# Transposes by halves of the rows, two score buffers, another order of the first loads and a logit sum by a product, in a fused attention and mixture-of-experts kernel

## The chip, the cores and the metric

The kernel runs on one core of a Trainium2 chip. The metric is the device time of one execution, in microseconds. Engines are named as in the profile: PE is TensorE (matrix products; PEld are its weight loads), DVE is VectorE, ACT is ScalarE, POOL is GpSimd, SP is SyncE, which only issues DMA transfers. PSUM is the memory into which TensorE writes, eight banks of 128 partitions by 512 floats; VectorE and ScalarE read it.

## What is computed

The input is `q`, `k`, `v` of shape (8 batches, 8 heads, 576 positions, 64). Attention is local: each head's positions are cut into 9 chunks of 64, and a chunk attends only to itself. The result, 4608 tokens of 512 features, goes through a mixture of 8 experts in which an expert keeps at most `capacity` = 80 tokens, those with the largest gate weight.

```python
scores = scale * np.matmul(q_c, k_c.transpose(0, 1, 2, 4, 3))   # per chunk of 64
attn = np.exp(scores - np.max(scores, axis=-1, keepdims=True))
attn = attn / (np.sum(attn, axis=-1, keepdims=True) + 1e-09)
x = np.matmul(attn, v_c)                  # then (batch, position) x (head, feature)
...
logits = x @ w_gate
expert_idx = np.argmax(logits, axis=1)
gate_w = probs[np.arange(N), expert_idx]
for e in range(E):
    tok_idx = np.where(expert_idx == e)[0]
    if len(tok_idx) > capacity:
        tok_idx = tok_idx[np.argpartition(-gate_w[tok_idx], capacity)[:capacity]]
    h = np.maximum(x[tok_idx] @ w1[e], 0.0)
    out[tok_idx] = gate_w[tok_idx, None] * (h @ w2[e])
```

## The kernel before

**Stages.** First comes the attention loop, over 36 units of 128 tokens with all 8 heads. Then follows a stretch in which the last gate weights are worked out and, for each expert, the tokens above its threshold are found and put in order (the tail). Then come six rounds of expert products, each on 128 slots, with the expert weights arriving by DMA; the results are scattered to the output rows. The other output rows are written with zeros.

**One unit.** `load(i)` issues the DMA transfers of unit i: queries (256 KB) and, in two halves, keys and values (258 KB each). Keys and values stand in one of seven buffers `kvb`; only the odd or the even partitions of each half are ever loaded, and the rest must be zero, so all seven buffers are zeroed once at the start. `scores(i)` multiplies queries by keys into PSUM (eight products of 128 rows by 64 columns, which appear as 16 instructions since each is done in two passes); VectorE takes the maximum of each row (L322) and subtracts it (L325), which gives `sm`. `probs(i)` transposes `sm` on TensorE, four transposes of 128 by 128 (L336) into one PSUM bank, and ScalarE takes the exponential from there (L338). `values(i)` multiplies by the values (L356), and VectorE normalises (L363 to L367) into `x`. `xtrans(i)` transposes `x`, again four transposes of 128 by 128 (L388) into a bank of its own, and ScalarE copies the result to `xT` (L389).

**Order of the work.** The order on each engine is that of the program text, written by hand. Pass i of the loop issues `scores(i)`, `probs(i-1)`, `values(i-2)`, `xtrans(i-3)` and the loads of unit i+5, so four units are under way at once. After each fourth unit `gate_mm`, `gate_copy` and `gate_sum` work out the logits of four units: the gate weights stand in four groups of 32 columns, one for each quarter of the features, and the four partial logits must be summed. `gate_sum` transposes them (L421), and VectorE sums the four parts (L425). What follows on the logits (maximum, exponential, key; `gate`) is put into a queue `gates`, and the search for each expert's threshold into a queue `bounds_q`; `fill()`, which is called five times in a unit, issues one step of the first and two of the second between the VectorE instructions of the unit. Some of these steps are ScalarE activations: the counts of the key search (`search_count`, L570, three rounds of two) and the level counts (`signs`, L504).

**PSUM.** Of the eight banks, scores have two (the loop uses one of them, one buffer), transposed probabilities one (`pt`), transposed `x` one (`m`), values two (`o`), and the gating two buffers of one bank (`g`).

**Start.** The seven buffers are zeroed first (L738: four on VectorE, three on GpSimd), then unit 0 is loaded, then VectorE zeroes `warm` (L742), on which TensorE does 14 products so that its clock comes up (`warm_up`, L747), then the other loads and constants follow. A product that needs zeros or data waits for them by semaphore.

**Tail.** After the loop the last four units of `x` are transposed (L388), the last two of them into the two halves of one tile of two banks; then the logits of the last eight units, the counts, the mask and the ranks follow, mostly one after the other.

Of the kernel before, what the change touches and what calls it, by code (L numbers as in the profile page):

```python
# [8 lines left out]
F32 = mybir.dt.float32  # L9
# [22 lines left out]
NWARM = 14  # L32
# [26 lines left out]
NCONST = C_V3 + 3  # L59
# [3 lines left out]
def attention_moe(ctx: ExitStack, tc: tile.TileContext, q, kv, wg, w1, w2, cap, cst, out):  # L63
# [20 lines left out]
    comp = cp.tile([P, RT, 6, NE], BF16, name="comp")  # L84
# [44 lines left out]
    def compact(pool, pp, ptok, tag):  # L129

        cand = pp.tile([P, 5, NE], F32, name=f"cand{tag}", tag="cand")
        for rt in range(RT):
# [4 lines left out]
                rhs=comp[:, rt, 0:5].rearrange("p c e -> p (c e)"),  # L137
# [129 lines left out]
    with ExitStack() as actx:  # L267
# [28 lines left out]
        def load(i):  # L296

# [7 lines left out]
            nc.sync.dma_start(t, q[T, r])  # L305
            for h in range(2):
                (nc.scalar if i < 2 and h else nc.sync).dma_start(kb[h:P:2, h], kv[T, r, h])

        def scores(i):
# [3 lines left out]
            ps = ps1.tile([P, 4, P], F32, name=f"s{i}", tag="s")  # L313
# [16 lines left out]

        def probs(i):
            d = U[i]
            pt = ps1.tile([P, 4, P], F32, name=f"pt{i}", tag="pt")
            sv = d['sm'].rearrange("p c k h -> p c (k h)")
            for pr in range(4):
                nc.tensor.transpose(pt[:, pr, :], sv[:, pr, :], ident)  # L336
            pT = wk.tile([P, 4, P], F32, name=f"pT{i}", tag="pT")
            nc.scalar.activation(pT, pt, AF.Exp, scale=0.125)  # L338
            d['pT'] = pT

        def values(i, last=False):
# [10 lines left out]
            po = ps1.tile([P, 2, 512], F32, name=f"o{i}", tag="s" if last else "o")  # L352
            for pr in range(4):
                o = 130 * (pr % 2)
                for u in range(2):
                    nc.tensor.matmul(  # L356
                        po[64 * u:64 * u + 64, pr // 2, o:o + 130].rearrange(
# [4 lines left out]
            pov = po[:, :, 0:260].rearrange("p j (m x) -> p j m x", m=4)  # L362
            nc.vector.tensor_scalar(rc, pov[..., 64], 1e-9, None, op0=ALU.add)  # L363
# [3 lines left out]
            nc.vector.tensor_tensor(  # L367
                t['x'][:, r, :].rearrange("p (j m e) -> p j m e", j=2, m=4), pov[..., 0:64],
                rc[:, :, :, None].to_broadcast([P, 2, 4, 64]), op=ALU.mult)
# [12 lines left out]
        def xtrans(i, pm=None):  # L382
            T, r = divmod(i, 4)
            t = TT[T]
            if pm is None:
                pm = ps1.tile([P, 4, P], F32, name=f"px{i}", tag="m")
            for pr in range(4):
                nc.tensor.transpose(pm[:, pr, :], t['x'][:, r, P * pr:P * pr + P], ident)  # L388
            nc.scalar.copy(t['xT'][:, :, P * r:P * r + P], pm)  # L389

        def gate_mm(rt, n):
            t = TT[rt // 4]
            U[rt]['pl'] = pls = []
            banks = ((ps2, "g"),) if rt < HALVES else ((ps2, "g"), (ps1, "m"))
            w = P * n // len(banks)
            for j, (pool, tag) in enumerate(banks):
# [339 lines left out]
        with tc.manual_schedule():  # L736
# [19 lines left out]
            for n in range(1, 4):  # L756
                load(n)
# [386 lines left out]
```

## Time and profile before

| | us |
|---|---|
| three runs | 274.03, 275.99, 277.04 (median 275.99) |
| the profiled execution, its own time | 273.62 |
| its span, first to last instruction | 271.4 |
| TensorE busy in it | 246.6 |
| VectorE busy | 134.7 |
| ScalarE busy | 77.5 |
| GpSimd busy | 55.2 |

In the rows of the timeline the first number is the start in microseconds from the start of the span, the second the duration (of the whole merged run of instructions where a row stands for several, x4 for instance), then come engine, line of the kernel, operation, output and inputs, and shapes. In brackets stands how long the engine had been idle before, and what released it. For TensorE the shapes are those of the stationary operand (rows by columns) and of the moving one. Rows by stretch give the busy time of each engine in the stretch, with the count of its instructions, TensorE's granted clock as a share of full speed, the busy share of the 16 DMA engines (up to about 1.04 is seen) and what they moved in GB/s. Grouped rows give the count, the busy time in all, the mean of one in ns, and the idle time before them with its cause.

### The profile page before, as it was taken

Reading aid. Unit: us, or ns where it says so; the run is one execution under the profiler, and the core shown is the slowest. Engines: PE = TensorE matmul, PEld = TensorE weight load, DVE = VectorE, ACT = ScalarE, POOL = GpSimd, SP = SyncE. Lnnn points to the kernel's source line nnn. Section 1 sums busy time; section 2 is a strip of 40 time slices with the busy share of each in tenths; the row PEclk is TensorE's granted clock in tenths of the full one; section 3 lists DMA queues with packets and bytes.
Section 4 is the critical chain, followed back from the end, with each engine's and each line's share of the span. In section 5 each row is a group of like instructions: output and inputs, shape, how many; then the busy total and the mean of one; then the engine's idle time right before and its main releaser. Section 6 shows DMA issues by size and latency. Waiting matters only on the chain. (4 is left out here: it accounts for less than half of the span.)

```text
span 271.4 us, 6612 instructions
## 1 busy us (share of the span) xinstructions
PE 246.6 (91%) x2703; PEld 148.9 (55%) x2703; DVE 134.7 (50%) x419; ACT 77.5 (29%) x159; POOL 55.2 (20%) x115
## 2 busy tenths in 40 slices
PE   0579999999999999999998878999999999999970
PEld 0458777777767687787876667342343434233320
DVE  7348758686767869695873867121121112112210
ACT  1003433433443554375755330220020202001000
POOL 9020101102020203069023453500000011110011
PEclk9999999999999999999999999999999999999996
DMA  4998799989998899979999971899999999996001
GB/s 145 381 282 294 250 323 386 347 280 315 390 341 315 278 342 318 378 261 391 395 408 408 331 297 44 295 368 406 404 393 408 407 403 393 407 387 244 0 36 35
DMA packets 32755, 84.71 MB, mean 312 GB/s; under 512 B 3344, under 2 KB 3472, under 8 KB 32720
## 3 DMA queue, kind: packets, MB, share of 16 engines
q1 hardware_dynamic: 28960, 71.32, 71.6%
q0 software_dynamic: 3456, 12.32, 13.0%
q10 hardware_dynamic: 304, 0.59, 0.6%
q8 instruction: 23, 0.38, 0.6%
q14 instruction: 12, 0.10, 0.1%
HBM read 64.04 MB, written 20.45 MB: 311 GB/s over the span
## 5 line engine op out<-in xcount | busy, mean ns | idle before, releaser
L202 PE MATMUL hc<-w,xtc 128*32 128x512 f32 x384 | 44.2, 594 | 0.2 <-ACT xtc L192 0.2
L235 PE MATMUL yc<-w,htc 128*32 128x512 f32 x384 | 43.4, 593 | 0.1
L316 PE MATMUL s<-kv,q 128*64 128x128 f32 x576 | 40.0, 282 | 1.8 <-POOL capc L768 1.7
L356 PE MATMUL o<-kv,pT 128*64 128x130 f32 x576 | 39.7, 279 | 0.0
L322 DVE TENSOR_REDUCE mx<-s 128x8 f32<-128x512 f32 x36 | 24.8, 690 | 22.4 <-PE s L316 22.3
L316 PEld LDWEIGHTS s<-kv,q 128*64 128x64 f32 x576 | 31.4, 138 | 8.3 <-issue 5.8
L356 PEld LDWEIGHTS o<-kv,pT 128*64 128x64 f32 x576 | 31.1, 135 | 5.9 <-issue 5.9
L338 ACT ACTIVATE pT<-pt 128x512 f32<-128x512 f32 x36 | 21.5, 597 | 35.1 <-PE pt L336 34.8
L235 PEld LDWEIGHTS yc<-w,htc 128*32 128x32 f32 x384 | 12.5, 110 | 29.2 <-issue 28.2
L202 PEld LDWEIGHTS hc<-w,xtc 128*32 128x32 f32 x384 | 12.1, 110 | 26.0 <-issue 25.6
L367 DVE TENSOR_TENSOR x<-o,rc 128x512 f32<-128x512 f32 x36 | 24.8, 689 | 0.8 <-DMA xs<-x 0.2
L325 DVE TENSOR_TENSOR sm<-s,mx 128x512 f32<-128x512 f32 x36 | 24.8, 690 | 0.6
L389 ACT COPY xT<-px 128x512 f32<-128x512 f32 x32 | 18.6, 581 | 22.1 <-PE px L388 22.0
L336 PE MATMUL pt<-ct,sm 128*128 128x128 f32 x144 | 23.5, 286 | 0.0
L388 PE MATMUL px<-ct,x 128*128 128x128 f32 x144 | 22.7, 283 | 0.8 <-ACT kv L389 0.8
L241 POOL DMA_INDIRECT out<-ysc,si x6 | 6.0, 995 | 84.8 <-DMA out<-zero 42.4
L207 ACT ACTIVATE hsc<-hc 128x512 f32<-128x512 f32 x6 | 3.6, 598 | 64.4 <-PE hc L202 64.4
L240 DVE TENSOR_SCALAR ysc<-yc,gatec 128x512 f32<-128x512 f32 x6 | 4.5, 752 | 34.5 <-PE yc L235 34.5
L336 PEld LDWEIGHTS pt<-ct,sm 128*128 128x128 f32 x144 | 15.1, 140 | 10.2 <-issue 9.5
L388 PEld LDWEIGHTS px<-ct,x 128*128 128x128 f32 x144 | 15.4, 141 | 5.1 <-issue 4.0
L463 POOL TENSOR_TENSOR comp<-comp,ct 128x32 bf16<-128x32 bf16 x18 | 3.9, 234 | 61.0 <-DVE comp L477 61.0
L209 DVE TENSOR_SCALAR hsc<-hc 128x512 f32<-128x512 f32 x6 | 4.1, 691 | 22.9 <-PE hc L202 22.9
(160 smaller groups left out, 242.3 us busy)
## 6 DMA issues: line engine op xcount, KB each, us to landing
w<-in_w SPq DMA_DIRECT2D x12, 2048.0 KB, 20.2
kv<-in_kv SPq DMA_DIRECT2D x70, 258.0 KB, 4.9
q<-in_q SPq DMA_DIRECT2D x36, 256.0 KB, 5.3
out<-zero SPq DMA_DIRECT2D x9, 1024.0 KB, 18.2
xs<-x POOLq DMA_DIRECT2D x8, 1024.0 KB, 7.1
w<-in_w SPq DMA_DIRECT2D x8, 1024.0 KB, 8.5
xs<-x POOLq DMA_DIRECT2D x4, 256.0 KB, 8.3
kv<-in_kv ACTq DMA_DIRECT2D x2, 258.0 KB, 4.2
```

The lines of the kernel that those rows point to most:

```text
L202: nc.tensor.matmul(h[o:o + 32, :], lhsT=xT[r][:, b, o:o + 32], rhs=getw(groups[r][g])[0][:, b, 512 * f:512 * f + 512], start=(b == 0), sto ...
L235: nc.tensor.matmul(y[o:o + 32, :], lhsT=hT[r][c // 4][:, c % 4, o:o + 32], rhs=getw(groups[r][g])[1][:, c, :], start=(c == 0), stop=(c == ...
L241: nc.gpsimd.indirect_dma_start(out=out, out_offset=bass.IndirectOffsetOnAxis(ap=si[:, r:r + 1], axis=0), in_=ys, in_offset=None, bounds_ch ...
L316: nc.tensor.matmul(ps[64 * u:64 * u + 64, pr, :].rearrange("p (h k) -> p h k", h=2), lhsT=t['q'][:, pr, u, :], rhs=t['k'][:, :, pr, u, :], ...
L322: nc.vector.tensor_reduce(mx, s8, axis=AX.X, op=ALU.max)
L325: nc.vector.tensor_tensor(sm.rearrange("p c k h -> p c h k"), s8, mx[:, :, :, None].to_broadcast([P, 4, 2, 64]), op=ALU.subtract)
L336: nc.tensor.transpose(pt[:, pr, :], sv[:, pr, :], ident)
L338: nc.scalar.activation(pT, pt, AF.Exp, scale=0.125)
L356: nc.tensor.matmul(po[64 * u:64 * u + 64, pr // 2, o:o + 130].rearrange("p (h x) -> p h x", h=2), lhsT=d['pT'][:, pr, 64 * u:64 * u + 64], ...
L367: nc.vector.tensor_tensor(t['x'][:, r, :].rearrange("p (j m e) -> p j m e", j=2, m=4), pov[..., 0:64], rc[:, :, :, None].to_broadcast([P, ...
L388: nc.tensor.transpose(pm[:, pr, :], t['x'][:, r, P * pr:P * pr + P], ident)
L389: nc.scalar.copy(t['xT'][:, :, P * r:P * r + P], pm)
```

## The change

*Transposes.* A new function `halves` does each group of four transposes as eight: for each quarter the upper 64 and the lower 64 partitions apart, 64 moving columns each, the upper ones into the first, the lower ones into the second of a pair of banks. Probabilities and `x` share that one pair (tag `tp`); ScalarE reads both banks in one instruction. *Scores* have two buffers of one bank. *Logits:* the transposes and VectorE's sum of the four parts become one product for each unit with a constant matrix of ones and zeros (`C_SUM`, eight columns), and the next steps read the logits from PSUM. *Start:* the queries of unit 0, the identity and the zeroing of `warm` come first, the buffer of unit 0 is zeroed in two halves on two engines, the loads of unit 0 follow, and `warm_up` does 24 products instead of 14. *Gating:* the exponential of the gate is issued one step after the subtraction that feeds it, for all but the last two groups, and the one-hot mask moves out of `comp` into a tile `mine`. *Tail:* the last four transposes go into four separate tiles (two by halves, two as before), and other late tiles move to the new buffers.

```diff
-NWARM = 14
+NWARM = 24
...
-            ps = ps1.tile([P, 4, P], F32, name=f"s{i}", tag="s")
+            ps = ps1.tile([P, 4, P], F32, name=f"s{i}", tag="s", bufs=2)
...
+        def halves(src, nm, tag="tp"):
+
+            pm = ps1.tile([P, 2, 512], F32, name=nm, tag=tag)
+            for pr in range(4):
+                for u in range(2):
+                    rows = slice(64 * u, 64 * u + 64)
+                    nc.tensor.transpose(pm[:, u, 64 * pr:64 * pr + 64], src(pr)[rows],
+                                        ident[rows, rows])
+            return pm[:, :, 0:256].rearrange("p u (a j) -> p a u j", a=4)
+
         def probs(i):
             d = U[i]
-            pt = ps1.tile([P, 4, P], F32, name=f"pt{i}", tag="pt")
             sv = d['sm'].rearrange("p c k h -> p c (k h)")
-            for pr in range(4):
-                nc.tensor.transpose(pt[:, pr, :], sv[:, pr, :], ident)
+            pt = halves(lambda pr: sv[:, pr, :], f"pt{i}")
             pT = wk.tile([P, 4, P], F32, name=f"pT{i}", tag="pT")
-            nc.scalar.activation(pT, pt, AF.Exp, scale=0.125)
+            nc.scalar.activation(pT.rearrange("p a (u j) -> p a u j", u=2), pt, AF.Exp,
+                                 scale=0.125)
...
-        def xtrans(i, pm=None):
+        def xtrans(i, tag="tp"):
             T, r = divmod(i, 4)
             t = TT[T]
-            if pm is None:
-                pm = ps1.tile([P, 4, P], F32, name=f"px{i}", tag="m")
-            for pr in range(4):
-                nc.tensor.transpose(pm[:, pr, :], t['x'][:, r, P * pr:P * pr + P], ident)
-            nc.scalar.copy(t['xT'][:, :, P * r:P * r + P], pm)
+            dst = t['xT'][:, :, P * r:P * r + P]
+            if tag == "s":
+                pm = ps1.tile([P, 4, P], F32, name=f"px{i}", tag="s", bufs=2)
+                for pr in range(4):
+                    nc.tensor.transpose(pm[:, pr], t['x'][:, r, P * pr:P * pr + P], ident)
+            else:
+                pm = halves(lambda pr: t['x'][:, r, P * pr:P * pr + P], f"px{i}", tag)
+                dst = dst.rearrange("p a (u j) -> p a u j", u=2)
+            nc.scalar.copy(dst, pm)
...
         def gate_sum(rt, n):
             lt = U[rt]['lt']
-            pm = ps2.tile([P, n, 4, 32], F32, name=f"lT{rt}", tag="g")
+            lg = ps2.tile([P, n, NE], F32, name=f"lT{rt}", tag="g")
             for c in range(n):
-                nc.tensor.transpose(
-                    pm[:, c].rearrange("p a b -> p (a b)"),
-                    lt[c * len(lt) // n][:, P * (c % (n // len(lt))):][:, 0:P], ident)
-            lg = gk.tile([P, n, NE], F32, name=f"lg{rt}", tag="lg")
-            gates.append((lambda: nc.vector.tensor_reduce(
-                lg, pm[:, :, :, 0:8].rearrange("p c g e -> p c e g"), axis=AX.X, op=ALU.add), ()))
+                nc.tensor.matmul(
+                    lg[:, c, :], lhsT=lt[c * len(lt) // n][:, P * (c % (n // len(lt))):][:, 0:P],
+                    rhs=ct[:, C_SUM:C_SUM + NE], start=True, stop=True)
             gate(rt, n, lg, gates)
...
             def shifted():
                 v.tensor_tensor(sh, lg, m[:, :, None].to_broadcast(bc), op=ALU.subtract)
+                if rt >= 28:
+                    raised()
+
+            def raised():
                 nc.scalar.activation(ex, sh, AF.Exp)
...
+            if rt < 28:
+                fns[3:3] = [raised]
...
         with tc.manual_schedule():
-            for j, kb in enumerate(kvb):
-                (nc.vector if j % 2 == 0 else nc.gpsimd).memset(kb, 0.0)
-            load(0)
+            load_q(0)
             nc.scalar.dma_start(ident, cst[:, C_ID:C_ID + P])
             warm = gk.tile([P, 2 * P], BF16, name="warm", tag="lv", bufs=LV)
             nc.vector.memset(warm, 0.0)
+            for j, kb in enumerate(kvb):
+                if j:
+                    (nc.gpsimd, nc.vector)[j % 2].memset(kb, 0.0)
+                else:
+                    nc.vector.memset(kb[:, 0], 0.0)
+                    nc.gpsimd.memset(kb[:, 1], 0.0)
+            nc.vector.memset(wgp[:, :, 8:32], 0.0)
+            load_q(1)
+            load_kv(0)
...
             warm_up(NWARM)
-            nc.vector.memset(wgp[:, :, 8:32], 0.0)
...
-            for n in range(1, 4):
+            load_kv(1)
+            for n in range(2, 4):
                 load(n)
...
-            xtrans(32)
-            xtrans(33, ps1.tile([P, 4, P], F32, name="px33", tag="pt"))
-            px = ps1.tile([P, 2, 4, P], F32, name="px34", tag="s")
-            xtrans(34, px[:, 0])
-            xtrans(35, px[:, 1])
+            for rt, tag in ((32, "tp"), (33, "s"), (34, "s"), (35, "o")):
+                xtrans(rt, tag)
...
+    c[:, C_SUM:C_SUM + NE] = p % 32 == np.arange(NE)[None, :]
```

More of the change, by code (lines that the diff above doesn't have):

```diff
@@ L351, in values @@
             t = TT[T]
-            po = ps1.tile([P, 2, 512], F32, name=f"o{i}", tag="s" if last else "o")
+            if last:
+                po = [ps1.tile([P, 1, 512], F32, name=f"o{i}_{j}", tag="s", bufs=2)
+                      for j in range(2)]
+                bank, parts = (lambda j: po[j][:, 0]), [(slice(j, j + 1), po[j]) for j in range(2)]
+            else:
+                po = ps1.tile([P, 2, 512], F32, name=f"o{i}", tag="o")
+                bank, parts = (lambda j: po[:, j]), [(slice(0, 2), po)]
             for pr in range(4):
@@ L366, in values @@
             fill()
[L367 to L369 removed]
+            xv = t['x'][:, r, :].rearrange("p (j m e) -> p j m e", j=2, m=4)
+            for js, pov in parts:
+                w = [P, js.stop - js.start, 4, 64]
+                nc.vector.tensor_tensor(xv[:, js], pov[..., 0:64],
+                                        rc[:, js, :, None].to_broadcast(w), op=ALU.mult)
             fill()
@@ L393, in gate_mm @@
             U[rt]['pl'] = pls = []
-            banks = ((ps2, "g"),) if rt < HALVES else ((ps2, "g"), (ps1, "m"))
-            w = P * n // len(banks)
-            for j, (pool, tag) in enumerate(banks):
-                pl = pool.tile([P, w], F32, name=f"L{rt}_{j}", tag=tag)
+            banks = 1 if rt < HALVES else 2
+            w = P * n // banks
+            for j in range(banks):
+                pl = (ps1.tile([P, 2, 512], F32, name=f"L{rt}_{j}", tag="tp")[:, 0, 0:w] if j else
+                      ps2.tile([P, w], F32, name=f"L{rt}_{j}", tag="g"))
                 for pr in range(4):
@@ L867, in attention_moe @@
                                          mask.rearrange(fl), 0.0, op0=ALU.mult, op1=ALU.add)
-            two = ps1.tile([P, 2, 512], F32, name="two", tag="s")
-            pos = two[:, 0, 0:NE * RT].rearrange("p (e r) -> p e r", e=NE)
+            two = [ps1.tile([P, 512], F32, name=f"two{j}", tag="s", bufs=2) for j in range(2)]
+            pos = two[0][:, 0:NE * RT].rearrange("p (e r) -> p e r", e=NE)
             for i, (a, b) in enumerate(((tr_b, mask), (idp, mask), (ones_b, inc))):
```

66 lines of the change are left out of this document (39 added, 27 removed).

## The prediction

> **What bounds the kernel now.** I read the page first, then busy time by stretch, then TensorE's timeline, stretch by stretch, and last the waits at the two ends. The page puts TensorE far ahead of the rest; the stretches say what else is near its limit.
>
> ```profile
> span 271.4 us, 6612 instructions
> ## 1 busy us (share of the span) xinstructions
> PE 246.6 (91%) x2703; PEld 148.9 (55%) x2703; DVE 134.7 (50%) x419; ACT 77.5 (29%) x159; POOL 55.2 (20%) x115
> ```
>
> ```profile
> core 0: us, PE busy (x) PEld busy (x) DVE busy (x) ACT busy (x) POOL busy (x), PEclk, DMA share, GB/s
> 24.78:138.56 113.78, 113.60 (x1416) 86.27 (x1415) 85.94 (x283) 52.67 (x109) 26.01 (x65) 1.00 0.94 333
> 84.00:138.56 54.56, 54.38 (x707) 41.68 (x707) 43.64 (x172) 29.59 (x67) 18.08 (x40) 1.00 0.93 335
> 190.00:210.00 20.00, 20.00 (x188) 6.78 (x184) 2.89 (x4) 1.74 (x3) 0.00 (x0) 1.00 1.04 402
> ```
>
> The first stretch runs from the scores of unit 4 to those of unit 35, the attention loop. TensorE has no gap there at full clock. VectorE is at 76% (80% in the second half), ScalarE at 46%, and the DMA engines at 0.94 where the expert stage reaches 1.04, so they have little to spare.
>
> ```profile
> 24.78 1.09 PE L316 MATMUL s<-kv,q 128*64 128x128 f32 x16
> 25.81 0.66 PE L336 MATMUL pt<-ct,sm 128*128 128x128 f32 x4
> 26.39 1.11 PE L356 MATMUL o<-kv,pT 128*64 128x130 f32 x16
> 27.43 0.66 PE L388 MATMUL px<-ct,x 128*128 128x128 f32 x4
> 28.02 1.09 PE L316 MATMUL s<-kv,q 128*64 128x128 f32 x16
> ...
> 38.13 0.66 PE L421 MATMUL lT<-ct,lt 128*128 128x128 f32 x4
> 38.63 0.60 PE L388 MATMUL px<-ct,x 128*128 128x128 f32 x4
> ```
>
> Start to start, a unit takes 3.24 us: scores 1.03, four transposes 0.58, values 1.04, four transposes 0.59. So the loop's bound is TensorE's own issue, and each of its two transpose groups is 18% of a unit. The four of L421, followed by more of the same kind, take 38.63 - 38.13 = 0.50; four followed by another kind take 0.59. So a group is 4 x 0.11, about 0.05 for its first weight load, and 0.09 of draining where the tile shape changes: 0.15 of overhead.
>
> **The change part by part.** *Transposes by halves.* A group's 4 instructions of 128 rows become 8 of 64 rows, each with 128 stationary and 64 moving columns, in turn on the upper and the lower rows, into two banks. The trace has two instructions of exactly that shape, but both on the same rows:
>
> ```profile
> 110.99 0.27 PE L619 MATMUL pb<-ct,lo 64*128 64x64 f32 x1
> 111.10 0.22 PE L619 MATMUL pb<-ct,km 64*128 64x64 f32 x1
> 111.25 0.33 PE L421 MATMUL lT<-ct,lt 128*128 128x128 f32 x1
> ```
>
> ```profile
> 110.99 0.13 PEld L619 LDWEIGHTS pb<-ct,lo 64*128 64x128 f32 x1 [0.17 <-issue]
> 111.04 0.13 PEld L619 LDWEIGHTS pb<-ct,km 64*128 64x128 f32 x1
> ```
>
> ```profile
> 103.90 0.14 PEld L316 LDWEIGHTS s<-kv,q 128*64 128x64 f32 x2 [0.17 <-issue]
> ```
>
> Each is a single pass (x1), so a half stays one instruction. The second load starts 0.05 after the first; the second product starts 0.11 after the first (one load and one stream of 0.055), and the next kind follows 0.15 later (0.055 and 0.09). A half thus costs 0.055. What no row shows is whether an upper and a lower half run side by side. Bounds: in turn, 8 x 0.055 + 0.15 = 0.59, no gain; in pairs, 4 x 0.055 + 0.15 = 0.37, a gain of 0.22. The nearest row is the last: the two column tiles of the scores start their loads together, and the 16 instructions take 1.03, less the 0.15 that is 0.055 apiece, where each streams 128 columns for 0.11, so tiles of one array do overlap there. I take 0.22. The Trainium skill, in "TensorEngine Tiling (Array Packing)", section "Key Properties", says that different tiles can load weights and multiply in parallel, which gives the same 0.22; no run here shows it for rows.
>
> In the loop's 31 periods stand 62 groups: 62 x 0.22 = 13.6 us. Against it: the logit sum (7 in the loop) becomes plain products, two passes each by the pattern of L316's 16 for 8, so 8 loads of 0.055 instead of 4 x 0.11, the same; but it no longer shares its tile shape with the group behind it, 0.15 more each, 1.0. The tallies and the key transposes, which now change shape too, cost about 1.0 in six places. Between 0 and 3 for both together; I take 2.0.
>
> *One pair of banks for both kinds of group.* Each group now waits until ScalarE has read the group before it, where each kind had its own bank.
>
> ```profile
> 139.58 0.66 PE L336 MATMUL pt<-ct,sm 128*128 128x128 f32 x4
> ```
>
> ```profile
> 140.34 0.60 ACT L338 ACTIVATE pT<-pt 128x512 f32<-128x512 f32 x1 [0.26 <-PE pt L336]
> ```
>
> ```profile
> L389 ACT COPY xT<-px 128x512 f32<-128x512 f32 x32 | 18.6, 581 | 22.1 <-PE px L388 22.0
> L504 ACT ACTIVATE lv<-io_b,bo 128x256 bf16<-128x256 bf16 x23 | 10.4, 500 | 4.1 <-DVE bo L499 4.0
> ...
> L425 DVE TENSOR_REDUCE lg<-lT 128x32 f32<-128x128 f32 x9 | 2.5, 281 | 0.1
> ```
>
> An idle ScalarE starts 0.76 after the group starts; with halves 0.54. Its pass takes 0.60, the release about 0.17 (the scores of unit 1, below). So the pair is free 1.31 after a group starts, and TensorE comes back after 0.37 + 1.04 = 1.41. The cover is 0.10 us. Queued behind each wait on TensorE are the scores or values of the whole unit. ScalarE has 1.41 - 0.60 = 0.81 between its passes, room for one of the other 0.50 us operations. The key search (three rounds of two, I price them like L504) and the level counts of five tiles (four each) put two or three of them ahead of one copy or exponential, 0.2 to 0.7 over: eight places at 0.4 are 3.2. VectorE in the second half would have 43.6 - 1.1 (four of L425's reductions) of about 49 us, 87%, and be late here and there, 0.8. I take 4 us of stalls, bounds 0 and 10 (0.16 for every group). The loop then gives 13.6 - 2.0 - 4.0 = 7.6, and lasts 106.2. The DMA engines need 0.94 x 113.8 / 1.04 = 103 for what they move in it, so this just fits. The exponential that is put one step later costs nothing: ScalarE's queue then holds no operation whose input VectorE hasn't begun.
>
> *Start.*
>
> ```profile
> L738 DVE MEMSET kv<- 128x2064 f32 x4 | 7.1, 1778 | 2.4 <-PEq L1133 1.2 <-issue 1.1
> ```
>
> ```profile
> 9.46 0.17 DVE L742 MEMSET warm<- 128x128 uint32 x1
> 9.60 0.14 DVE L749 MEMSET wgp<- 128x96 f32 x1
> 14.52 0.69 DVE L322 TENSOR_REDUCE mx<-s 128x8 f32<-128x512 f32 x1 [4.79 <-PE s L316]
> 15.25 0.69 DVE L325 TENSOR_TENSOR sm<-s,mx 128x512 f32<-128x512 f32 x1
> ```
>
> ```profile
> 9.68 3.17 PE L747 MATMUL pw<-warm 128*128 128x256 bf16 x14 [9.68 <-DVE warm L742]
> 12.78 1.69 PE L316 MATMUL s<-kv,q 128*64 128x128 f32 x16
> 16.14 1.09 PE L316 MATMUL s<-kv,q 128*64 128x128 f32 x16 [1.67 <-POOL capc L768]
> 17.17 0.55 PE L336 MATMUL pt<-ct,sm 128*128 128x128 f32 x3
> ```
>
> ```profile
> 3.04 0.58 SPq L307 DMA_DIRECT2D kv<-in_kv  x1
> ```
>
> ```profile
> DMA to landing us min/median/max: 2.9/4.2/5.9
> ```
>
> These are, in turn, VectorE's zeroing as a group, the start on VectorE and on TensorE, and the issue of the first keys, with the time that such loads take to land.
>
> The first key load is issued at 3.04 and would land near 7.2, but TensorE's warm-up waits for a zeroing that stands behind four of 1.78 on VectorE, so the scores start at 12.78. After the change VectorE does that one first (1.2 + 0.17), then half a buffer (0.4 + 0.89): the load goes at 2.7, lands near 6.9 (8.6 at the slowest landing shown), and the 24 warm-up products (3.1 us for 14 here) start near 1.7 and lie under it. Three zeroings of 1.78 with gaps of 0.38 (1.1 over three) follow on VectorE, so the maximum that was at 14.52 comes at 2.7 + 6.5 + 0.1 = 9.3. Unit 1's scores, which wait until 16.14 for VectorE to finish reading the one score buffer (15.25 + 0.69 = 15.94; the releaser named had no part), no longer do. The first group of transposes then starts at 9.3 + 2 x 0.73 + 0.2, near 10.9, instead of 17.17, and at the old pace (24.78 - 17.17, less 3 x 0.22) unit 4's scores come at 17.9, 6.9 earlier. I take 6.5, since the loads of units 1 to 4 are issued hardly sooner than before and have less time to land; bounds 4 (slow landings) and 7.
>
> *Tail and experts.*
>
> ```profile
> 144.85 1.56 ACT L389 COPY kv<-px 128x512 f32<-128x512 f32 x3 [1.90 <-PE px L388]
> ```
>
> ```profile
> 146.47 0.66 PE L388 MATMUL px<-ct,x 128*128 128x128 f32 x4 [0.82 <-ACT kv L389]
> ```
>
> The last transposes wait 0.82 for the copy out of the tile they share; with four separate tiles the copies run through, 0.7 less. One reduction of 0.28 leaves the chain, and one 0.22 is gained ahead of it: 1.2, between 0 and 2. The expert stage does the same work and its later weights are issued only after the tail, so it moves as a block.
>
> Sum: 6.5 + 7.6 + 1.2 = 15.3 us. The profiled execution took 273.62 (span 271.4); 273.6 - 15.3 = 258.3, a factor of 0.944. Its time lies 0.9% under the median shown, 275.99, which I take as the base: 260.5.
>
> **The rivals.** *Halves one after the other* (the change wouldn't do what it says). For it: both L619 halves are on the same rows and tell nothing of pairs. Against: the scores' column tiles. The loop loses 2.0 and about 1 of stalls, the start gives 6, the tail 0.8: 3.8 gained, 269.8, on the median's base 272.2.
>
> *The cover goes.* With 0.10 us of cover at each of 62 handovers, ScalarE at 29.6 of 49 us, VectorE at 87% and DMA at its floor, the wait for the shared pair, or a late VectorE, becomes the bound of the loop's second half. The loop then gives 2 instead of 7.6: 9.5 to 10 gained, 264, or 266.
>
> *A half costs load and stream in series.* If a half's weights can't be loaded under the stream of the other rows' half, a group takes 8 x 0.11 + 0.09 = 0.97, 0.38 more, in some 66 groups 25 us; less 4.5 from start, tail and changes of shape, 294. It decides from the point where a group costs 4.5 / 66 = 0.07 more than 0.59, about 64 ns a half. Against it: load and stream of L619's two overlap. The Trainium skill, "TensorE: Matmul & The Clock Gate", section "LDWEIGHTS (loading the stationary operand)", puts a load at columns over 1.2, an estimated 107 ns for 128 columns, which in series would make a group 1.0 us and the time about 296; the trace disagrees, with 0.05 from load to load.
>
> **How the numbers follow.** Forecast 0.56, cover gone 0.20, halves in turn 0.17, series 0.07. The range 254 to 271.5 leaves out the series case, half of the case in turn, and 0.05 below, where no stalls occur. A change under 1% (2.8 us) isn't told from none. Faster by more: the first two cases and half of the third, 0.85; within: most of the rest of the third, 0.07; slower: 0.08.
>
> **What would show it.** TensorE's timeline: a group start to next kind of 0.37 (0.59 or 0.97 otherwise), a unit of 2.8 in the first half of the loop; the waits: TensorE on ScalarE at the transposes, a few us in the second half, many in the second rival; first scores near 7 and unit 4's near 18. The prediction is wrong if pairs don't overlap, or if a unit stays above 3.1 with TensorE idle.

## The result, and the profile after

The changed kernel takes 265.12 us (median of four runs, 264.1 to 266.05), the kernel before, beside it, 276.51 (four runs, 274.03 to 277.43): a ratio of 0.960, with a 95% interval of 0.952 to 0.968. The forecast was 260.5, with a range of 254 to 271.5. The profiled execution took 264.55 (span 262.7), where that of before took 273.62 (271.4). Medians here and below are of all executions, but ratios and intervals leave out slow ones, more than 1.5% above the fastest of their kernel; two of the five of the logit sum by transposes are such, its profiled one among them, and its other three have a median of 258.94.

| first instruction of | before | after | gain since the row above | forecast |
|---|---|---|---|---|
| scores of unit 4 | 24.78 | 19.21 | 5.6 | 6.5 |
| scores of unit 35 | 138.56 | 129.76 | 3.2 | 7.6 |
| first expert product | 170.06 | 160.79 | 0.5 | 1.2 |
| end of the span | 271.4 | 262.7 | -0.6 | 0 |

The page and the busy time by stretch, for the changed kernel (columns as for the kernel before):

```profile
span 262.7 us, 7225 instructions
...
PE 243.0 (93%) x3029; PEld 150.3 (57%) x3029; DVE 131.8 (50%) x412; ACT 77.1 (29%) x159; POOL 56.2 (21%) x116
```

```profile
core 0: us, PE busy (x) PEld busy (x) DVE busy (x) ACT busy (x) POOL busy (x), PEclk, DMA share, GB/s
10.00:14.00 4.00, 3.98 (x34) 2.77 (x36) 1.38 (x2) 0.60 (x1) 0.00 (x0) 0.58 1.02 375
...
19.20:129.76 110.56, 107.78 (x1694) 85.67 (x1690) 84.55 (x277) 52.06 (x109) 26.05 (x65) 0.98 0.97 350
...
89.00:98.00 9.00, 7.01 (x92) 5.62 (x90) 7.03 (x31) 4.54 (x14) 1.52 (x8) 0.81 0.88 324
```

TensorE now has idle time in the loop (2.8 us), and TensorE's granted clock is below 1.00 in two stretches, 10 to 14 and 89 to 98 us. The timeline of one unit, and of the logit sum:

```profile
24.91 1.09 PE L326 MATMUL s<-kv,q 128*64 128x128 f32 x16
25.93 0.46 PE L347 MATMUL pt<-ct,sm 64*128 64x64 f32 x8
26.32 1.11 PE L381 MATMUL o<-kv,pT 128*64 128x130 f32 x16
26.50 0.60 ACT L356 ACTIVATE pT<-pt 128x512 f32<-128x512 f32 x1 [0.89 <-PE pt L347]
27.36 0.46 PE L347 MATMUL px<-ct,x 64*128 64x64 f32 x8
27.76 1.09 PE L326 MATMUL s<-kv,q 128*64 128x128 f32 x16
...
31.21 1.06 PE L455 MATMUL lT<-ct,lt 128*128 128x8 f32 x8
32.20 0.46 PE L347 MATMUL px<-ct,x 64*128 64x64 f32 x8
```

A group of transposes lasts 0.39 (25.93 to 26.32), where it lasted 0.58 to 0.59; a unit lasts 2.85. ScalarE is done at 27.10, and TensorE is back at 27.36. The logit sum of four units lasts 0.99 (31.21 to 32.20), twice what it was.

I added up, from the trace, the time from the first weight load of each kind of work to the first of the next kind, over the 31 periods of the loop; a wait falls to the kind that stands ahead of it:

| us in the loop | before | after | change |
|---|---|---|---|
| both groups of transposes | 36.8 | 24.8 | -12.0 |
| logit sums (7) | 2.7 | 6.9 | +4.2 |
| sums of level counts (tallies) and key transposes | 2.35 | 2.83 | +0.5 |
| scores and values, waits behind them included | 64.1 | 68.15 | +4.05 |
| all other | 7.8 | 7.8 | 0 |
| sum | 113.8 | 110.6 | -3.2 |

So the halves gave 12 us, and 8.8 were lost again. The scores and values themselves are no slower; most of what they lose is lost in one place, the key search. The timeline there, of ScalarE, VectorE and TensorE:

```profile
88.78 0.28 DVE L646 TENSOR_SCALAR nt<-ct,wd,lo 64x3 f32<-64x3 f32 x1
89.09 0.51 ACT L608 ACTIVATE sg<-kT,nt 64x256 bf16<-64x256 f32 x1 [1.56 <-DVE nt L646]
90.09 0.57 ACT L356 ACTIVATE pT<-pt 128x512 f32<-128x512 f32 x1
90.72 0.46 PE L347 MATMUL px<-ct,x 64*128 64x64 f32 x8 [1.41 <-ACT pT L356]
92.80 2.00 PE L381 MATMUL o<-kv,pT 128*64 128x130 f32 x16
95.36 1.39 PE L326 MATMUL s<-kv,q 128*64 128x128 f32 x16
95.72 0.51 ACT L608 ACTIVATE sg<-kT,nt 64x256 bf16<-64x256 f32 x1 [2.15 <-DVE nt L646]
97.33 0.47 PE L347 MATMUL pt<-ct,sm 64*128 64x64 f32 x8 [0.59 <-ACT xT L422]
```

The count `sg` stands at the head of ScalarE's queue and waits for `nt`, which VectorE works out late. The exponential behind it could have started soon after 88.2; it starts at 90.09. TensorE waits 1.41 for the shared pair, and soon afterwards its values take 2.00 where 1.11 is usual. Another 0.9 us is lost in the same way near 109 us, where a level count waits for VectorE's `bo` with an exponential behind it:

```profile
109.33 0.51 ACT L542 ACTIVATE lv<-io_b,bo 128x256 bf16<-128x256 bf16 x1 [1.21 <-DVE bo L537]
110.38 0.46 PE L347 MATMUL px<-ct,x 64*128 64x64 f32 x8 [0.44 <-ACT pT L356]
```

### The profile page after: what moved, and what is told of

Its sections match the earlier page's. It is cut to its first block, busy times and chain, and to the rows that moved or that the text cites. A ratio compares the mean times of both kernels' runs of the same rounds, so it can differ in the third digit from the quotient of the medians.

```text
span 262.7 us, 7225 instructions
## 1 busy us (share of the span) xinstructions
PE 243.0 (93%) x3029; PEld 150.3 (57%) x3029; DVE 131.8 (50%) x412; ACT 77.1 (29%) x159; POOL 56.2 (21%) x116
## 5 line engine op out<-in xcount | busy, mean ns | idle before, releaser
L381 PE MATMUL o<-kv,pT 128*64 128x130 f32 x576 | 40.5, 283 | 0.1
L332 DVE TENSOR_REDUCE mx<-s 128x8 f32<-128x512 f32 x36 | 24.8, 688 | 18.3 <-PE s L326 18.2
L381 PEld LDWEIGHTS o<-kv,pT 128*64 128x64 f32 x576 | 31.8, 137 | 2.6 <-DVE x L397 0.2
L397 DVE TENSOR_TENSOR x<-o,rc 128x512 f32<-128x512 f32 (+1 forms) x37 | 24.9, 675 | 1.5 <-DMA xs<-x 0.7
L347 PEld LDWEIGHTS pt<-ct,sm 64*128 64x128 f32 x288 | 12.0, 140 | 11.9 <-issue 9.5
L347 PE MATMUL pt<-ct,sm 64*128 64x64 f32 x288 | 17.0, 238 | 1.1 <-ACT xT L422 1.1
L347 PE MATMUL px<-ct,x 64*128 64x64 f32 x272 | 16.0, 237 | 2.0 <-ACT pT L356 1.8
L498 POOL TENSOR_TENSOR comp<-mine,ct 128x32 bf16<-128x32 bf16 x18 | 3.9, 234 | 57.5 <-DVE mine L512 57.5
L226 DVE COPY htc<-hpc 128x512 f32<-128x512 f32 x6 | 4.2, 692 | 22.0 <-PE hpc L222 22.0
```

What stands on the lines that cost most here:

```text
L332: nc.vector.tensor_reduce(mx, s8, axis=AX.X, op=ALU.max)
L347: nc.tensor.transpose(pm[:, u, 64 * pr:64 * pr + 64], src(pr)[rows], ident[rows, rows])
L381: nc.tensor.matmul(bank(pr // 2)[64 * u:64 * u + 64, o:o + 130].rearrange("p (h x) -> p h x", h=2), lhsT=d['pT'][:, pr, 64 * u:64 * u + 64 ...
L397: nc.vector.tensor_tensor(xv[:, js], pov[..., 0:64], rc[:, js, :, None].to_broadcast(w), op=ALU.mult)
```

## The experiments

Ratios are to the kernel before, measured on the same chip beside them (medians 274.09 to 274.61); the changed kernel's is 0.960. "Loop" is the time from unit 4's scores to unit 35's in the profiled execution, 110.6 for the changed kernel.

**Whole transposes, all else as changed.**

```diff
-                for u in range(2):
-                    rows = slice(64 * u, 64 * u + 64)
-                    nc.tensor.transpose(pm[:, u, 64 * pr:64 * pr + 64], src(pr)[rows], ident[rows, rows])
+                nc.tensor.transpose(pm[:, 0, P * pr:P * pr + P], src(pr), ident)
```

> The changed kernel with each group again as four transposes of 128 rows, into the first bank of the shared pair; one pair for both kinds as changed. Theory (halves run side by side, 0.39 us a group against 0.585): 62 groups in the loop cost 0.19 each, the loop rises from 110.6 by about 12 less what falls away of its 4.4 us of waiting, to 119 to 123, the whole to about 0.99 to 1.0 of the kernel before. Rival (the gain came from the other parts, and the groups' time is hidden by ScalarE or VectorE): the loop rises by less than 5 us.

Measured: 274.6 us, ratio 0.999 (0.994 to 1.004), loop 119.5. Its timeline:

```profile
26.45 0.66 PE L345 MATMUL pt<-ct,sm 128*128 128x128 f32 x4
27.03 1.11 PE L378 MATMUL o<-kv,pT 128*64 128x130 f32 x16
```

A group lasts 0.58 again, and the whole gain is gone: without the halves, the rest of the change is worth nothing in sum, the start's gain being spent on the logit sum and the waits. TensorE waits for the shared pair as in the changed kernel (2.1 us in the loop, 2.6 there).

**Upper halves first, then the lower.** Four upper halves are issued ahead of four lower ones.

```diff
-            for pr in range(4):
-                for u in range(2):
+            for u in range(2):
+                for pr in range(4):
```

> The changed kernel with the eight halves of a group in another order: the four of the upper rows first, then the four of the lower rows. Theory (two halves run side by side only where upper and lower ones follow each other): a group takes 0.5 to 0.6 us instead of 0.39, and the loop rises by 7 to 12 us. Rival (the halves are cheap on their own, or later ones are taken ahead of earlier ones): a group stays at about 0.39 and the time is that of the changed kernel, 0.96 of the kernel before.

Measured: 264.8 us, ratio 0.964 (0.957 to 0.971), loop 110.1. Its timeline:

```profile
26.02 0.47 PE L347 MATMUL pt<-ct,sm 64*128 64x64 f32 x8
26.42 1.11 PE L381 MATMUL o<-kv,pT 128*64 128x130 f32 x16
```

A group takes 0.40. Issue order inside a group of eight makes no difference: the trace still shows the loads in four pairs, 0.01 us apart in a pair and 0.06 from pair to pair. That neighbours must alternate is refuted; that the two row halves overlap is not, since eight loads in series at 0.055 would make 0.59. Which two halves form a pair can't be read from the trace. The two on the same rows in the kernel before (L619) did not run as one, with 0.05 from load to load and 0.11 from product to product, so I take a pair to be an upper and a lower half; but rows and banks change together here, and that the rows alone decide is not shown.

**The logit sum by transposes again.** The four transposes and VectorE's reduction stand in place of the product.

```diff
-                nc.tensor.matmul(lg[:, c, :], lhsT=lt[...], rhs=ct[:, C_SUM:C_SUM + NE], start=True, stop=True)
+                nc.tensor.transpose(pm[:, c].rearrange("p a b -> p (a b)"), lt[...], ident)
...
+            gates.append((lambda: nc.vector.tensor_reduce(lg, pm[:, :, :, 0:8]..., op=ALU.add), ()))
```

> The changed kernel with the old logit sum put back: four transposes of 128 by 128 for four units, and VectorE's reduction of their four parts; all else as changed. Theory (the product costs TensorE 0.11 us for each of its 8 passes, so a sum takes 0.99 us instead of 0.50): each of the 7 sums in the loop falls by 0.4 to 0.5 us, the stretch from unit 4's to unit 35's scores from 110.6 to about 107.5, the whole 3 to 4 us under the changed kernel, about 0.948 of the kernel before. Rival (the loop's time is set elsewhere, or VectorE's 0.28 us for each reduction comes back as waiting): the loop stays within 1 us of 110.6.

Measured: 259.95 us, ratio 0.941 (0.934 to 0.948), loop 106.7. Its timeline:

```profile
32.00 0.66 PE L455 MATMUL lT<-ct,lt 128*128 128x128 f32 x4
32.59 0.46 PE L347 MATMUL px<-ct,x 64*128 64x64 f32 x8
```

The sum lasts 0.59 and not 0.99: 0.40 for each of seven, 2.8 us of the loop. The other 1.0 or so is the lower clock of the changed kernel's one profiled execution: four versions whose loop has the same work and kept a clock of 1.00 (upper halves first, the old start, one score buffer, warm through the start) take 109.6 to 110.1. This version is faster than the changed kernel, since the intervals lie apart.

**The old start.** The order of zeroing, first loads and warm-up is that of the kernel before; all else is as changed.

```diff
-            load_q(0)
...
-            for j, kb in enumerate(kvb):
-                if j:
-                    (nc.gpsimd, nc.vector)[j % 2].memset(kb, 0.0)
...
+            for j, kb in enumerate(kvb):
+                (nc.vector if j % 2 == 0 else nc.gpsimd).memset(kb, 0.0)
+            load(0)
```

> The changed kernel with the old start: all seven buffers zeroed first, unit 0 loaded after that, 14 warm-up products. Theory (the start gives what the traces show at unit 4's scores): they come near 24 instead of 19.2 us, and the whole is 4.5 to 6 us above the changed kernel, about 0.98 of the kernel before. Rival (the earlier start is given back later, as the DMA engines are nearly full and the loads do not keep up): less than 2 us above the changed kernel.

Measured: 268.74 us, ratio 0.974 (0.966 to 0.982). Unit 4's scores start at 22.92, where the changed kernel has 19.21 and the kernel before 24.78. So the new order is worth 3.7 us in these executions, though the intervals of the two ratios just overlap. The other 1.9 come with the rest of the change: four faster groups ahead of unit 4, 0.8, and the first group of transposes, which starts 0.9 sooner (16.27 for 17.17) as the scores of units 0 and 1 now run back to back from 12.77.

**One score buffer.** An unused tile takes every second turn of the two buffers, so all scores but the last unit's use the same one.

```diff
+            if 0 < i < RT - 1:
+                ps1.tile([P, 4, P], F32, name=f"sx{i}", tag="s", bufs=2)
             ps = ps1.tile([P, 4, P], F32, name=f"s{i}", tag="s", bufs=2)
```

> The changed kernel, in which the scores of all units but the last use one of the two score buffers, as in the kernel before. Theory: at the steady pace VectorE frees the scores well before TensorE is back (in the kernel before TensorE waited for them only at the start), so the loop from unit 4 on stays at 110 to 111 us, and only the start is longer: scores of unit 1 wait for the subtraction of unit 0, unit 4's scores come 1 to 2 us later; ratio 0.962 to 0.967. Rival: with units of 2.85 us in place of 3.24 VectorE is late for the one buffer, some 0.1 to 0.2 us in each unit, and the loop grows by 3 to 6 us: ratio 0.972 to 0.985.

Measured: 263.67 us, ratio 0.958 (0.951 to 0.966), loop 109.6. Its timeline at the start, and its waits of TensorE in the loop (in all, times, longest):

```profile
6.57 1.09 PE L328 MATMUL s<-kv,q 128*64 128x128 f32 x16 [1.43 <-DMA kv<-in_kv]
9.16 1.09 PE L328 MATMUL s<-kv,q 128*64 128x128 f32 x16 [1.50 <-DMA kv<-in_kv]
10.19 0.46 PE L349 MATMUL pt<-ct,sm 64*128 64x64 f32 x8
10.58 1.05 PE L794 MATMUL pw<-warm 128*128 128x256 bf16 x8
...
17.53 1.09 PE L328 MATMUL s<-kv,q 128*64 128x128 f32 x16 [0.61 <-DMA kv<-in_kv]
```

```profile
PE px L349 <- ACT pT L358: 1.8, 2, 1.4
PE pt L349 <- ACT xT L424: 1.3, 2, 1.1
```

The second buffer is worth nothing that can be measured, neither in the loop, where no scores wait for VectorE, nor, with the new start, at the beginning, where unit 1's scores wait for their keys. My theory expected 1 to 2 us there, and unit 4's scores came 1.7 sooner instead, at 17.5: in this execution the clock did not drop at the start.

**Warm through the start.** In the changed kernel TensorE's timeline at the start was:

```profile
1.05 4.14 PE L792 MATMUL pw<-warm 128*128 128x256 bf16 x24 [1.05 <-DVE warm L778]
6.87 1.09 PE L326 MATMUL s<-kv,q 128*64 128x128 f32 x16 [1.68 <-DMA kv<-in_kv]
10.02 1.40 PE L326 MATMUL s<-kv,q 128*64 128x128 f32 x16 [2.05 <-DVE sm L335]
...
11.98 1.89 PE L792 MATMUL pw<-warm 128*128 128x256 bf16 x8
```

(The release by `sm` is an earlier event; the keys of unit 1, whose buffer is zeroed late, are the likelier cause.) The edit adds 10 products ahead of the scores of unit 0 and 16 behind them.

```diff
-NWARM = 24
+NWARM = 34
...
                 scores(i)
+                if i == 0:
+                    warm_up(16)
```

> The changed kernel, in which TensorE has 34 warm-up products in place of 24 ahead of the scores of unit 0, and 16 more between the scores of unit 0 and of unit 1, so that it is busy through the two waits at the start (1.68 and 2.05 us in the changed kernel). Nothing else is changed. Theory: the lower granted clock that the changed kernel shows from 10 to 14 us (0.58, where the 8 warm-up products take 1.89 in place of 1.05 and unit 2's scores come late) follows those two waits; with TensorE busy it stays at 1.00, the 16 products cost nothing because they end near 9.8, when the keys of unit 1 land, and unit 4's scores come at 17.3 to 18 in place of 19.2: time lower by 0.4 to 0.8%, ratio 0.953 to 0.957. Rival: the clock drops for another reason, or the landing of the keys alone sets the start; unit 4's scores stay at 19 or later, and the products that run over the landing cost up to 0.5 us.

Measured: 263.6 us, ratio 0.959 (0.954 to 0.964). Its timeline and busy time by stretch:

```profile
10.02 1.09 PE L326 MATMUL s<-kv,q 128*64 128x128 f32 x16
...
11.44 1.05 PE L792 MATMUL pw<-warm 128*128 128x256 bf16 x8
...
18.69 1.09 PE L326 MATMUL s<-kv,q 128*64 128x128 f32 x16 [0.93 <-DMA kv<-in_kv]
```

```profile
10.00:14.00 4.00, 4.00 (x59) 3.22 (x60) 1.83 (x3) 0.65 (x2) 0.00 (x0) 1.00 1.02 350
```

With TensorE busy the clock stays at 1.00, and the eight warm-up products take 1.05 and not 1.89. Of the 1.5 us that this saves, the late keys of unit 4 take back 0.93. That the added products kept the clock up is not shown by this alone, since in the version with one score buffer it stayed up without them. The time was to fall by 0.4 to 0.8%; the ratios differ by 0.15 points, within their intervals, so a gain in time is not shown.

**Search counts behind.** ScalarE's counts are kept in a list and issued only right behind the next exponential or copy.

```diff
             nc.scalar.activation(pT..., pt, AF.Exp, scale=0.125)
+            run_behind()
...
             nc.scalar.copy(dst, pm)
+            run_behind()
...
-                    nc.scalar.activation(sg, Z['kT'], AF.Sign, ...)
+                behind.append(both)       # both() issues the two activations
```

> The changed kernel, in which ScalarE's two activations of each round of the key search and the level counts are issued only right behind the next exponential or the next copy out of the shared pair; what is computed stays as it is. Theory: the stalls of the changed kernel's loop (about 4.4 us, nearly all between 88 and 98 us) come from the activations sg, which stand at the head of ScalarE's queue and wait 1.56 and 2.15 us for VectorE's nt, with an exponential or a copy that is ready behind them, so that TensorE waits for the shared pair (1.41 at 90.72) and then runs at a lower granted clock. Behind the copy they hold up nothing that is ready, the stretch 88 to 98 goes back to about 2.9 us a unit, and the loop of 110.6 becomes 106 to 107.5: time 0.945 to 0.95 of the kernel before. Rival: the wait only changes its place (sg still blocks the next copy while it waits for nt, and the search's rounds grow longer), the loop stays above 109.5, and the ratio at 0.957 or more.

Measured: 262.26 us, ratio 0.953 (0.946 to 0.960), loop 106.8. ScalarE's timeline:

```profile
89.56 0.60 ACT L362 ACTIVATE pT<-pt 128x512 f32<-128x512 f32 x1 [0.78 <-PE pt L347]
90.34 0.51 ACT L617 ACTIVATE sg<-kT,nt 64x256 bf16<-64x256 f32 x1 [0.18 <-DVE nt L656]
```

The exponential now runs first, the count waits 0.18, and from 20 to 136 us TensorE waits 0.5 in all. The loop's gain is as expected, but about 1.0 of the 3.8 is the changed kernel's lower clock, as above. In time it is 0.7 points, and the intervals overlap. In the profiled execution 1.4 of the 3.8 are taken back by the start (unit 4's scores at 20.6, again with a lower clock).

**Both.** The edits of the two versions "logit sum by transposes" and "search counts behind" together.

> The changed kernel with both edits: the logit sum by four 128 by 128 transposes and VectorE's reduction, as in the kernel before, and ScalarE's search and count activations right behind the next exponential or copy. Theory that the two losses add: the sum by product costs 3.8 us of loop (106.7 against 110.6), the waits of the search 3 to 4, so that the loop takes 103 to 104 and the time is 0.93 of the kernel before. Rival: the DMA engines become the bound, since they need an estimated 103 us for what they move in the loop (0.94 of 113.8 us, at the 1.04 of the expert stage): then the loop stops at 104.5 to 106, scores wait on q or kv in its second half, and the ratio is 0.937 to 0.945.

Measured: 259.62 us, ratio 0.942 (0.936 to 0.948), loop 106.7. The two gains of 3.8 do not add. Each of them holds the lower clock's 1.0, but counted from 109.6, too, they are 2.8 and 2.9 and would give 103.9. No scores wait for a transfer, so the rival fails as well. TensorE's waits:

```profile
PE pc L630 <- DVE rc L397: 0.7, 1, 0.7
PE pk L583 <- DVE keys L500: 0.7, 1, 0.7
PE pt L347 <- ACT xT L429: 0.7, 2, 0.3
PE ph L571 <- ACT lv L553: 0.4, 2, 0.2
```

They are waits for the small steps of the search, which stand in TensorE's queue earlier than VectorE, with one step more in its gating, gets to them.

**Both, and another start.** The sixth buffer is zeroed by GpSimd, the second by halves on both engines, and there are 34 warm-up products.

```diff
-                if j:
-                    (nc.gpsimd, nc.vector)[j % 2].memset(kb, 0.0)
+                if j > 1:
+                    (nc.gpsimd, nc.vector)[j == 3].memset(kb, 0.0)
                 else:                       # by halves, on VectorE and GpSimd
```

> As the kernel with both edits (sum by transposes, search behind), and a different order of the start: the zeroing of the second buffer is split between VectorE and GpSimd like the first's, the sixth's goes to GpSimd, and the warm-up has 34 products in place of 24. Theory: VectorE's zeroing ends an estimated 2.6 us sooner (1.78 for the sixth buffer, 0.89 for half the second), the maximum of unit 0 no longer waits for it (8.57 in the changed kernel, against scores that end near 7.9), the second unit's keys are issued 0.9 sooner, and TensorE doesn't idle from 5.2 to 6.8, so that its granted clock stays up; unit 4's scores come 1 to 1.5 us sooner than 19.2 and the time is 0.4 to 0.6% below that of the kernel with both edits. Rival: the loads of units 1 to 4 set the pace of the start, unit 4's scores stay within 0.5 us, and the two kernels differ by less than 0.2%.

Measured: 258.3 us, ratio 0.942 (0.936 to 0.947). Unit 4's scores start at 17.41 with the clock at 1.00, the loop is 106.7. The profiles differ as the theory says; the medians differ by 0.5%, the intervals overlap.

**Small steps later.** One step more ahead of the key transposes and of each of the search's three sums, two sums of levels in another order.

```diff
-                        gates.append((search_keys, ()))
+                        gates.extend([wait, (search_keys, ())])
...
-                bounds_q.extend([wait] * 7)
+                bounds_q.extend([wait] * 8)
...
-LEVELS = {..., 19: "l4:5 - s3 s0 c4", 23: "l5:6 s4 s1 c5", ...}
+LEVELS = {..., 19: "l4:5 s0 - s3 c4", 23: "l5:6 s1 - s4 c5", ...}
```

> The fastest version so far (sum by transposes, search behind, other start), with the steps on which TensorE still waited in its loop put later in the work that is handed out between units: the key transposes and each of the search's three sums one step later, two sums of levels behind a sum whose counts are long done, the last tile's counts no longer behind an exponential. Theory: the loop's remaining loss against the sum of both edits (106.7 us, where 3.8 and 3.8 less than 110.6 would give 103) is made up of waits of TensorE on VectorE and ScalarE for these small steps (0.7, 0.7, 0.7, 0.6 us), and goes: loop 104.5 to 105.5, time 0.4 to 0.8% below 258.3. Rival: the steps only collide with others, because VectorE (84.4 us of 106.7) and ScalarE's queue, or the DMA engines at a share of 0.98, set the pace; the loop stays within 0.7 us of 106.7.

Measured: 258.3 us, ratio 0.939 (0.934 to 0.944), loop 103.3. TensorE has 0.6 us of waits left in it; about 0.7 of the 3.4 is only work that now falls behind unit 35's scores (one of the five sums of levels). So the two edits do add in the loop, once the small steps are out of the way. The time stays the same: the stretch from unit 35's scores to the first expert product is 32.7 in place of 30.6, and unit 4's scores came at 19.1, since a wait of 2.15 ahead of unit 1's scores was again followed by a lower clock (0.66 from 10 to 15 us).

**The last mended too.** 14 products behind the scores of unit 0, and the last counts, which the version before had put back to where they were, behind the exponentials like the others.

```diff
                 scores(i)
+                if i == 0:
+                    warm_up(14)
...
-                    (signs if T == 6 else lambda j: behind.append(...), (4 * T + r,))
+                    (lambda j: later(lambda: signs(j)), (4 * T + r,))   # later: behind, up to the last exponential
```

> The version with later sums, changed in two places. The counts of the last tile but one go behind the exponentials like the others, up to the last exponential, and 14 warm-up products stand between the scores of unit 0 and of unit 1. Theory: the version with later sums lost what its loop gained (103.3 us from unit 4's to unit 35's scores) at both ends; in the tail a count at the head of ScalarE's queue waited 2.26 us for VectorE with the exponential of unit 34 behind it and TensorE waited 1.00 for that, so 32.7 us in place of 30.6 from unit 35's scores to the first expert product; at the start TensorE waited 2.15 us and then ran at a lower granted clock, so unit 4's scores came at 19.1 in place of 17.4. With both mended the loop stays at 103 to 104, the tail comes to 30.5 to 31.5, unit 4's scores to 17.3 to 18.7, and the time to 0.5 to 1.2% below 258.3: ratio 0.928 to 0.934. Rival: the tail's 2 us belong to the small steps that now run out later, whichever way the counts are queued, and the time stays within 0.3% of 258.3.

Measured: 259.44 us, ratio 0.944 (0.940 to 0.949). Unit 4's scores come at 17.39 and the loop is 103.3, as expected, but the next stretch is 34.0. The first expert product starts at 154.65; in the two versions above it started at 154.70 and 155.09, though unit 35's scores began at 120.64 here and at 124.09 and 122.38 there. VectorE's timeline and the busy time by stretch of this version:

```profile
123.42 0.69 DVE L407 TENSOR_TENSOR x<-o,rc 128x512 f32<-128x512 f32 x1 [2.65 <-DMA xs<-x]
```

```profile
112.00:124.00 12.00, 10.72 (x208) 8.89 (x203) 8.11 (x35) 7.82 (x17) 5.18 (x17) 1.00 1.03 397
```

VectorE may not write `x` before an older tile of `x` has been stored to `xs`. That store is issued at 112.49 and lands some 11 us later, with the DMA engines full (share 1.03). TensorE's waits behind unit 35's scores come to 2.5 (1.20 for that `x`, 0.68, and three of 0.2); with the 0.7 of moved work they are most of the 3.4 by which the stretch is longer than 30.6. In the expert stage one product waits 1.5 for its weights, where the two versions above wait 0.2 at most. Neither my theory (ScalarE's queue) nor its rival (the small steps) named this. The version with later sums shows the same wait (1.82), the one before it does not. I read this as the DMA engines setting the end of the loop once it is faster than about 106 us. It is not shown: no run tried the store by itself, and the share from 112 to 124 us is 1.03 in the version before the later sums too, where nothing waits. The order of the transfers is an untested rival, since four 1 MB writes of zeros are issued from 110.81, ahead of the store.

No combination beats 258.3 us, which two versions reach: 2% below the changed kernel by the ratios (0.939 and 0.942 against 0.960). Nor is any of them shown to be faster than the logit sum by transposes alone, at 0.941 with an interval of 0.934 to 0.948.

## Why the prediction was right, and where it was not

The direction, the pairing of the halves and the range held; the point was 1.8% low, 15.3 us of gain forecast where the spans differ by 8.7. The terms below account for the difference, the logit sum for the largest part of it. Step by step:

*Halves run in pairs*: right, and it is the whole of the gain, as the version with whole transposes shows. A group was priced at 0.37 and took 0.39, since a pair takes 0.06 and not 0.055: 12.0 us in place of 13.6.

*The logit sum "the same"*: this term was mis-sized, and it is the largest miss. I took eight loads of 0.055 from transposes. As a plain product each of the eight passes takes 0.112 ((0.99 - 0.09) / 8). The profile's group of its weight loads shows the difference too, 191 ns for one against 140 for the transposes':

```profile
L347 PEld LDWEIGHTS pt<-ct,sm 64*128 64x128 f32 x288 | 12.0, 140 | 11.9 <-issue 9.5 <-ACT xT L422 2.1 <-ACT io_b L811 0.2
...
L455 PEld LDWEIGHTS lT<-ct,lt 128*128 128x128 f32 x72 | 8.6, 191 | 1.4 <-ACT pT L356 0.7 <-ACT lt L446 0.4 <-DVE left L685 0.2
```

The sum cost 4.2 us in the loop where 1.0 was allowed: 2.8 for the passes, which the version with the sum by transposes gives back, and 1.4 for the change of shape. The Trainium skill, "TensorE: Matmul & The Clock Gate", section "LDWEIGHTS (loading the stationary operand)", gives columns over 1.2, an estimated 107 ns for 128 columns. I set that aside because transposes show 0.055; for this product the trace agrees with it.

*Tallies and key transposes*: 0.5, where 1.0 was allowed.

*Cover of 0.10 for the shared pair*: right. ScalarE ends at 27.10 and TensorE is back at 27.36; less the 0.17 of a release, 0.09 is left, and in a plain unit nothing waits.

*Stalls of 4 us*: right in size (4.05) by luck, wrong in kind. I expected eight places where ScalarE has too much to do between two passes. There are two of any size, in the key search, and a small one near 109 us; at each ScalarE has nothing to do, since its queue is held by a count whose input VectorE hasn't finished. Such waits cost nothing before, when each kind of transposes had its own bank. They stood in the trace of before, with an exponential behind the count, while TensorE had no gap:

```profile
99.55 0.51 ACT L570 ACTIVATE sg<-kT,nt 64x256 bf16<-64x256 f32 x1 [1.57 <-DVE nt L608]
```

I had looked for a waiting operation at the head of ScalarE's queue only for the exponential that the change moves, and not for the counts that it leaves in place. About 1.4 of the 4.05 (0.9 on the values at 92.80, the rest on the next transposes and scores) is the lower clock, which I hadn't foreseen. It also shortens the next wait: versions with the same search and a clock of 1.00 wait 1.1 where this one waits 0.59, so its net price is 0.5 to 1.0.

*Start*: the order of events was right: unit 0's scores at 6.87 (forecast near 7). Unit 1's scores, forecast not to wait, waited 2.05, most likely for their keys. Unit 4's came at 19.21, not 18.3, because of the two waits and the clock behind them; with TensorE kept busy they come at 17.4 to 18.7. (At the old pace four groups of transposes stand ahead of unit 4's scores, not the three that I took off.)

*Tail*: 1.2 forecast, 0.5 measured. The wait of 0.82 went, but the last eight units' logit sum takes 1.81 (139.23 to 141.04) where it took 0.96, and the reduction that VectorE no longer does gives back only part of that.

```profile
139.23 1.95 PE L455 MATMUL lT<-ct,lt 128*128 128x8 f32 x16
141.04 2.78 PE L734 MATMUL pwarm<-io_b,ones_b 128*128 128x256 bf16 x24
```

*Experts as a block*: nearly; the stage grew by 0.6, of which 0.4 is a wait for weights. *DMA floor of 103 us for the loop*: not contradicted, and not tested. The two last versions reach 103.3 and 103.2, but TensorE is busy for 102.7 of that, so its own work still sets the pace there.

Of the rivals, halves in turn and load and stream in series are refuted by the group of 0.39. The time measured, 265.1, is nearer to the rival of the lost cover (266) than to the forecast, and so is the loop's gain, 3.2 (2 in the rival, 7.6 in the forecast). But that mechanism isn't there: in the loop's second half TensorE waits at four places and not at every handover, and moving the counts removes these waits without any more cover. The largest part of the loop's shortfall is the logit sum, which the rival didn't have either.

## What to carry to other kernels

When two consumers' buffers are merged into one, look at every operation ahead of the consumer in its queue, above all at those the edit doesn't touch: one that waits for a third engine was free while the buffer was private, and now stops the producer. Price a product by a row of a product and a transpose by a row of a transpose, even where shape and type are the same. And once the bound engine has been sped up, check what else is near its limit: here the DMA engines were at 0.94 before and at 0.99 to 1.01 once the loop was some 10 us shorter, and the fastest loops gave no better time.

## What the runs showed that I had not expected

*The order of row halves doesn't matter*: alternating, or four upper and then four lower, a group takes 0.39 or 0.40.

*The clock can halve behind short waits, and not always.* The granted clock, as a mean over each stretch, fell to 0.58 (10 to 14 us) behind waits of 1.68 and 2.05, to 0.66 behind one of 2.15, and the values took 2.00 in place of 1.11 some 2 us behind a wait of 1.41. But in the version with one score buffer it stayed at 1.00 behind waits of 1.43 and 1.50, and behind the same wait of 1.41 in the key search. In finer stretches it is 0.50: in the changed kernel from 10.7 to 14.0 and from 92.6 to 96.0 us, in the version with search counts behind from 9.2 to 16.0. The Trainium skill, "TensorE: Matmul & The Clock Gate", section "What's actually happening", has the clock fall after an idle window of about 3.4 us, with windows that run freely. No wait here is that long, so the length of the waits doesn't agree; that the lower clock lasts about 3.4 us or twice that, and that the same code is hit in one execution and not in the next, does. With products between the scores of units 0 and 1 the clock stayed up in both versions profiled; without them, among the versions with the new start, it fell in seven of nine. Two executions are few, and what exactly sets it off stays open.
